# Scalings and operand making moved from ScalarE and GpSimd to VectorE, seven products reordered, loads reissued in another order

## Chip, cores and metric

One core of a Trainium2 chip. TensorE (PE) multiplies matrices, VectorE (DVE), ScalarE (ACT) and GpSimd (POOL) work elementwise, SyncE (SP) starts transfers. Each engine executes its own instructions strictly in the order in which they were written, and waits where an instruction's operands or its target are not ready. The metric is the device time of one execution in microseconds, the median of several runs; lower is better.

## What is computed

Four sequences, eight heads, 576 positions of 64 features go through causal attention with a memory term; its output, seen as 2304 rows of 512 features, goes through four experts, all of which act on every row, weighted by probabilities.

```
a = softmax(causal(scale * q @ k.T));  local = a @ v
mem_out = (phi(q) @ M_prev) / (phi(q) @ z_prev + 1e-6)
x = g * mem_out + (1 - g) * local          # rows: 4 x 576, features: 8 heads x 64
p = domain_probs / domain_probs.sum(-1)
out = sum over e of  p[:, e] * (relu(x @ w1[e]) @ w2[e])    # 512 -> 1024 -> 512
```

## The kernel before

Numbers are kept in fp32. A product of the experts is made of three matmuls: each operand is split into a high half (`...h`, rounded) and a low half (`...l`, what the rounding left), and high·high, low·high and high·low are summed. So every operand costs one rounding copy and one subtraction on some engine before PE can use it.

**Expert phases.** The four experts' weights come in 8 halves of 512 hidden features, and the kernel goes through them in 32 phases. In phases 0 to 23 one or two groups of 256 rows are resident. A phase first makes h = x @ w1 for four blocks `fc` of 128 hidden features (`mm1`: 12 matmuls a block), with relu on ACT (`hh`, L836) and the low half on DVE (`hl`, L837), then y = h @ w2 (`mm2`: 12 matmuls of 512 columns for 128 rows) and adds y into `acc`. The groups become resident as attention finishes them, so attention and phases are interleaved: attention's steps are sorted by (slot, priority), and a planner places them between the parts of the phases by costs.

**Attention.** The first run of eight heads is made ahead (`first_run`). Then twelve joint tasks (two heads, 256 query rows) of four slots each, and after them tasks of single heads. A task loads q, k and v (`t_load`, into one of two sets of `natall` that alternate from task to task), transposes them (`tk`, `tp` on PE), makes scores, subtracts the maximum, exponentiates, sums (`j_sum`, L497 and L500: 1/sum into `st`), scales the scores `s` by `st` (`j_norm`, L506), transposes them to `pt`, copies these to `pth` (ACT) and `ptl` (DVE, L527), and multiplies by v (`o`). The result goes through `otmp` (ACT) into `xr` (DVE).

**Weights.** `w_dma` fills one of four stage buffers `stg` on SP's queue, and waits there for the buffer to come free; `w_prep` makes of it the high half (ACT or POOL, L240 and L242) and the low half (POOL, in some phases DVE, L244), and calls `w_dma` for the next.

**Tail.** Phases 24 to 31 work on the last 1024 rows at once. x and w1 are cut into 2 x 2 blocks, and x @ w1 is made in seven products instead of eight. `x_ops` makes the seven left operands A11, S1, S2, A12, S3, S4, A22 (sums at L970, high halves on ACT at L962, low halves at L963), a step at a time between the parts of phases 22 and 23, where DVE and POOL both make odd and even low halves of weights too. `wt_prep` makes the right ones: four sums `tsum`, three high halves on ACT (L1000 to L1002), three low halves `wtl`. `tail_mm1` then runs the seven products in two halves p of a phase; each is six matmuls into a PSUM bank X, Y or Z, and later products are added into the bank's earlier sum. ACT keeps the first three in `trow`; then each add (L1041), relu (L1037) and `hl` or `xl` (L1038) gives one of four blocks of h. `tail_mm2` makes y from h: 96 matmuls (`yt`), in which a pair of row tiles takes blocks 0 and 2 of the hidden features first and blocks 1 and 3 after. The line that ties the products to the elementwise work in the kernel before is

```
add(product("A12", 1, "Z"), 0, 0, p)      # DVE add, then ACT relu, then DVE low half
add(product("S3", 5, "X"), 1, 1, p + 2)
```

Of the kernel before, what the change touches and what calls it, by code (L numbers as in the profile page):

```python
# [58 lines left out]
def tile_attention_moe(  # L59
# [145 lines left out]
    wpos = {"dma": 0, "prep": 0}  # L205
# [19 lines left out]

    def w_prep(i, kind, pool=False):
        last_ = PH0 - 3 <= i < PH0
        act = (kind == "1" or i < START[1] or last_) and not pool
        j = wpos["prep"]
        if j >= len(wseq) or wseq[j][0] != i or wseq[j][1] != kind:  # L230
            return
        wpos["prep"] += 1
        fc = wseq[j][2]
        t = stg.pop(j)
        hi, lo = (w1s if kind == "1" else w2s)[fc]
        if kind == "1":
            hi = hi.rearrange("p c f -> p (c f)")
            lo = lo.rearrange("p c f -> p (c f)")
        if act:
            nc.scalar.activation(hi, t, AF.Copy)  # L240
        else:
            nc.gpsimd.tensor_scalar(hi, t, 1.0, 1.0, ALU.mult, ALU.mult)  # L242
        dve = (last_ and fc % 2) or (i < START[1] and fc < PR["lod"])
        (nc.vector if dve else nc.gpsimd).tensor_tensor(lo, t, f(hi), ALU.subtract)  # L244
        w_dma()
# [48 lines left out]
    def t_load(t):  # L294
        for n, src, c0 in (("q", q, t.cs[0]), ("k", k, 0), ("v", v, 0)):
            nfull = min(t.nk, NCH - 1) - c0
            for j in range(2):
                s_ = src[t.b, 2 * t.a + j]
                nc.sync.dma_start(
                    out=t.nat[n][:, 0:nfull, j],  # L300
                    in_=s_[c0 * P : (c0 + nfull) * P].rearrange("(c p) d -> p c d", p=P),
                )
            if t.nk == NCH:
                for r in {"q": (D,), "k": (0,), "v": (0, D)}[n]:
                    nc.sync.dma_start(
                        out=t.nat[n][r : r + S - 4 * P, nfull],
                        in_=src[t.b, 2 * t.a : 2 * t.a + 2, 4 * P : S].rearrange(
                            "h p d -> p h d"
                        ),
                    )  # L310
# [191 lines left out]
    def j_norm(i):  # L502
        s = slots[i]
        r = s.st[:, 4:6]
        for hd in range(2):
            nc.scalar.activation(s.s3[:, hd], s.s3[:, hd], AF.Copy, scale=r[:, hd : hd + 1])  # L506
# [223 lines left out]
    for t in tasks:  # L730
# [7 lines left out]
        ev(ld, 8, lambda t=t: t_load(t))  # L738
# [10 lines left out]
    for i, s in slots.items():  # L749
        w = wid(s.c)  # L750
        t = s.t
        if t.joint:
            ev(i, PQ["qk"], lambda i=i: j_qk(i), 4 * mm(w))
            ev(i, PQ["exp"], lambda i=i: j_exp(i))
            ev(i + PQ["jn"][0], PQ["jn"][1], lambda i=i: j_sum(i))
            ev(i + PQ["jn"][0], PQ["norm"], lambda i=i: j_norm(i))
# [160 lines left out]
    tail = {}  # L917
# [37 lines left out]
    def x_ops():  # L955
# [9 lines left out]
        def plain(n, i, k):  # L965
            return [lambda: put(n, a_blk(i, k), nc.gpsimd)]

        def summed(n, eng, dst, a, b, op):
# [8 lines left out]
            + summed("S2", nc.vector, s_, s_, a_blk(0, 0), ALU.subtract)  # L977
            + plain("A12", 0, 1)
            + summed("S3", nc.gpsimd, s3, a_blk(0, 0), a_blk(1, 0), ALU.subtract)
            + summed("S4", nc.vector, s_, a_blk(0, 1), s_, ALU.subtract)  # L980
# [3 lines left out]
    def wt_prep(i):  # L984

        j = wpos["prep"]
        if j >= len(wseq) or wseq[j][0] != i or wseq[j][1] != "1":
            return
        wpos["prep"] += 2
# [5 lines left out]
        gp = nc.gpsimd.tensor_tensor  # L995
# [10 lines left out]
        w_dma()  # L1006
        w_dma()

    def tail_mm1(i, p):
# [25 lines left out]
        def done(src, blk, fc):  # L1035
            h_, l_ = tail["h"][blk][0][fc], tail["h"][blk][1][fc]
            nc.scalar.activation(h_, src, AF.Relu)  # L1037
            nc.vector.scalar_tensor_tensor(l_, src, 0.0, f(h_), ALU.max, ALU.subtract)  # L1038

        def add(o, n, blk, fc):  # L1040
            nc.vector.tensor_tensor(r[:, n], o, r[:, n], ALU.add)  # L1041
            done(r[:, n], blk, fc)
# [4 lines left out]
        add(product("A12", 1, "Z"), 0, 0, p)  # L1047
        add(product("S3", 5, "X"), 1, 1, p + 2)
        add(product("S4", 2, "Y"), 2, 0, p + 2)
        done(product("A22", 6, "X"), 1, p)  # L1050
# [387 lines left out]
```

## Time and profile before

| | |
|---|---|
| median of 3 runs | 1077.06 us (1076.23 to 1078.12) |
| the profiled execution | 1077.43 us, of which the span from its first to its last instruction 1075.5 |
| granted clock of TensorE, mean | 0.981 of full speed |
| PE, DVE, ACT, POOL busy | 1003.5, 654.3, 567.6, 544.5 us |
| phases 0 to 23 with attention | up to about 730 us |
| phases 24 to 31 (tail) | from there to the end |

Busy times add up what an engine's instructions took, so the engine with the largest share is near its limit, and the others wait for it or for each other. The table says nothing of where in time the waits stand; the views below do. In a view of waits, "PE o L541 <- DVE ptl L527" reads: PE stood at its instruction of line 541, which writes `o`, until DVE's instruction of line 527, which writes `ptl`, was done.

### The profile page before, as it was taken

The numbers are of one execution on the slowest core, as the hardware profiler recorded it, in microseconds if no ns is written. First come the engines' busy times: TensorE is split into PE (matmuls) and PEld (weight loads), VectorE is DVE, ScalarE is ACT, GpSimd is POOL, SyncE is SP. The second block draws the span as 40 slices with busy tenths as digits, with TensorE's granted clock in tenths as the row PEclk, the third lists the DMA queues.
The fourth block names the chain that finished last, engine by engine and source line by source line (L and its number), as shares of the span: only waits on it lengthen the run. The fifth ranks groups of instructions, "written<-read, shape, count | busy, mean of one in ns | idle before, by whom it ended". The sixth has DMA issues, their size and how long they took to land.

```text
span 1075.5 us, 15732 instructions
## 1 busy us (share of the span) xinstructions
PE 1003.5 (93%) x5072; PEld 827.8 (77%) x5072; DVE 654.3 (61%) x1555; ACT 567.6 (53%) x1299; POOL 544.5 (51%) x592
## 2 busy tenths in 40 slices
PE   5787889979999999999999999978999999999998
PEld 3576767768888788888878888856877877878776
DVE  5666766677677677777667776564444444533533
ACT  4476856767666666767656666543232241332320
POOL 4657765465465466546475354378325235235220
PEclk8999989999999999999999999979999999999999
DMA  6545653545454445335543342434111112112002
GB/s 135 121 123 152 163 142 96 131 122 139 104 131 112 110 106 153 105 108 129 150 110 92 102 105 85 119 98 118 51 47 60 40 46 72 40 40 79 24 16 78
DMA packets 192513, 106.33 MB, mean 99 GB/s; under 512 B 99632, under 2 KB 170800, under 8 KB 192432
## 3 DMA queue, kind: packets, MB, share of 16 engines
q1 hardware_dynamic: 191760, 105.07, 36.2%
q8 instruction: 40, 0.66, 0.3%
q10 hardware_dynamic: 672, 0.27, 0.1%
q14 instruction: 41, 0.34, 0.1%
HBM read 90.09 MB, written 4.72 MB: 88 GB/s over the span
## 4 chain that ended last, share of the span: by engine, by line
PE 69%; DVE 13%; ACT 6%; issue 4%; POOL 4%; DMA 2%; SPq 1%; POOLq 0%; DVEq 0%; ACTq 0%
PE yt L1063 16%; PE y L857 15%; PE h L827 13%; PE o L708 3%; PE tc_1X L1022 3%; PE sp L597 3%; PE tc_0X L1022 3%; PE pt L345 3%; DVE trow L1041 2%; DVE hl L837 1%; POOL w2l L244 1%; DVE hl L1038 1%; DMA natall<-in_k_dram 1%; ACT hh L836 1%; PE tc_0Z L1022 1%
## 5 line engine op out<-in xcount | busy, mean ns | idle before, releaser
L244 POOL TENSOR_TENSOR w1l<-stg,w1h 128x512 fp32r<-128x512 f32 x90 | 116.8, 1303 | 160.6 <-ACT w1h L240 153.3
L244 POOL TENSOR_TENSOR w2l<-stg,w2h 128x512 fp32r<-128x512 f32 x122 | 160.7, 1317 | 28.7 <-ACT w2h L240 17.7
L827 PE MATMUL h<-xh,w1h 128*128 128x512 f32 (+1 forms) x384 | 149.9, 390 | 0.0
L827 PE MATMUL h<-xh,w1l 128*128 128x512 f32 (+1 forms) x384 | 139.5, 363 | 3.1 <-POOL w1l L244 3.1
L857 PE MATMUL y<-w2h,hh 128*128 128x512 f32 x320 | 138.1, 432 | 0.8 <-ACT w2h L240 0.8
L827 PE MATMUL h<-xl,w1h 128*128 128x512 f32 (+1 forms) x384 | 138.8, 361 | 0.0
L857 PE MATMUL y<-w2l,hh 128*128 128x512 f32 x320 | 128.0, 400 | 3.9 <-POOL w2l L244 3.3
L857 PE MATMUL y<-w2h,hl 128*128 128x512 f32 x320 | 128.2, 401 | 0.9 <-DVE hl L837 0.9
L837 DVE SCALAR_TENSOR_TENSOR hl<-h,hh 128x512 fp32r<-128x512 f32 (+1 forms) x96 | 57.7, 601 | 83.7 <-ACT hh L836 83.0
L1076 DVE SCALAR_TENSOR_TENSOR xt<-yt,pn,xt 128x512 f32<-128x512 f32 x56 | 42.0, 751 | 80.8 <-PE yt L1063 80.8
L640 ACT ACTIVATE s<-s,st 128x384 f32<-128x384 f32 (+2 forms) x80 | 55.0, 688 | 66.5 <-DVE st L635 66.4
L242 POOL TENSOR_SCALAR w2h<-stg 128x512 fp32r<-128x512 f32 x100 | 63.5, 635 | 45.3 <-PE yt L1063 45.3
L827 PEld LDWEIGHTS h<-xh,w1l 128*128 128x128 f32 x384 | 74.5, 194 | 14.4 <-POOL w1l L244 3.3
L827 PEld LDWEIGHTS h<-xh,w1h 128*128 128x128 f32 x384 | 74.9, 195 | 6.5 <-issue 0.2
L827 PEld LDWEIGHTS h<-xl,w1h 128*128 128x128 f32 x384 | 75.1, 196 | 5.5
L857 PEld LDWEIGHTS y<-w2h,hl 128*128 128x128 f32 x320 | 61.1, 191 | 14.9 <-DVE hl L837 1.2
L857 PEld LDWEIGHTS y<-w2l,hh 128*128 128x128 f32 x320 | 61.6, 192 | 13.6 <-POOL w2l L244 5.4
L873 DVE SCALAR_TENSOR_TENSOR acc<-y,pn,acc 128x512 f32<-128x512 f32 x70 | 52.3, 747 | 30.1 <-PE y L857 29.1
L1003 POOL TENSOR_TENSOR wtl<-stg,wth 128x512 fp32r<-128x512 f32 x16 | 20.9, 1306 | 97.6 <-ACT wth L1000 97.6
L836 ACT ACTIVATE hh<-h 128x512 fp32r<-128x512 f32 (+1 forms) x96 | 50.3, 524 | 36.3 <-PE h L827 35.3
L857 PEld LDWEIGHTS y<-w2h,hh 128*128 128x128 f32 x320 | 61.5, 192 | 9.5 <-ACT w2h L240 1.3
L646 DVE TENSOR_TENSOR ptl<-pt,pth 128x384 fp32r<-128x384 f32 (+1 forms) x96 | 51.8, 553 | 20.4 <-ACT pth L644 19.7
(294 smaller groups left out, 2635.6 us busy)
## 6 DMA issues: line engine op xcount, KB each, us to landing
stg<-in_moe_w_dram SPq DMA_DIRECT2D x256, 256.0 KB, 2.9
natall<-in_k_dram SPq DMA_DIRECT2D x34, 128.0 KB, 2.8
natall<-in_v_dram SPq DMA_DIRECT2D x32, 128.0 KB, 2.6
natall<-in_q_dram SPq DMA_DIRECT2D x60, 64.0 KB, 2.6
out_dram<-acc SPq DMA_DIRECT2D x10, 256.0 KB, 2.2
kha<-kha SPq DMA_DIRECT2D x16, 128.0 KB, 3.4
khb<-khb SPq DMA_DIRECT2D x16, 128.0 KB, 3.2
natall<-in_k_dram SPq DMA_DIRECT2D x28, 64.0 KB, 2.5
```

What stands on the lines that cost most here:

```text
L242: nc.gpsimd.tensor_scalar(hi, t, 1.0, 1.0, ALU.mult, ALU.mult)
L244: (nc.vector if dve else nc.gpsimd).tensor_tensor(lo, t, f(hi), ALU.subtract)
L640: nc.scalar.activation(s.s[:, 0:w], s.s[:, 0:w], AF.Copy, scale=s.st[:, 3:4])
L646: lambda x=x: nc.vector.tensor_tensor(x[2], x[0], f(x[1]), ALU.subtract) for x in groups
L827: nc.tensor.matmul(pt[0][:, cols], lhsT=w_[:, c], rhs=x_[:, c, cols], start=(c == 0 and z == 0), stop=(c == NKD - 1 and z == 2),)
L836: nc.scalar.activation(h_, pt[0][:, cols], AF.Relu)
L837: nc.vector.scalar_tensor_tensor(l_, pt[0][:, cols], 0.0, f(h_), ALU.max, ALU.subtract)
L857: nc.tensor.matmul(pt[0], lhsT=h_[fc][:, tk], rhs=w_, start=(fc == 0 and z == 0), stop=(fc == HF - 1 and z == 2),)
L873: nc.vector.scalar_tensor_tensor(acc[g, tt], pt[0], pe, acc[g, tt], ALU.mult, ALU.add)
L1022: nc.tensor.matmul(bank[b][:, 0:TB], lhsT=w_[:, n, cs], rhs=x_[:, c], start=first and c == 0 and z == 0, stop=c == 1 and z == 2, skip_grou ...
L1063: nc.tensor.matmul(o, lhsT=h_[fc][:, tk], rhs=w_, start=(z == 0 and fc == p and y == 0), stop=(z == 1 and fc == p + 2 and y == 2),)
L1076: nc.vector.scalar_tensor_tensor(acc_, o, pe, acc_, ALU.mult, ALU.add)
```

## The change

- `j_norm`: the scaling of the joint scores is two tensor_scalar instructions on DVE, issued directly after `j_sum`, where it was two activations on ACT, issued later in the same slot.
- `x_ops`: the low halves of A11, A12 and A22 and both steps of S3 are made on DVE, where they were on POOL, and the operands are made in the order A11, S1, S2, S4, S3, A12, A22.
- `wt_prep` for phase 24 alone: the sums and the first `wtl` on DVE, where they were on POOL.
- `tail_mm1`: products in that order too; the relus are issued directly behind the adds, and the low halves later.
- Weight loads are counted as due when a preparation is issued, and issued ahead of the next preparation (`w_more`).
- `t_load` is called twice: for q and k at slot s0 − 9 of a task that starts at slot s0, for v at s0 − 7. Before, all three were loaded at s0 − 7 (s0 − 9 for the first task).

```diff
+    def w_more():
+        while wpos["due"]:
+            wpos["due"] -= 1
+            w_dma()
...
     def w_prep(i, kind, pool=False):
...
+        w_more()
         wpos["prep"] += 1
...
-        w_dma()
+        wpos["due"] += 1
...
-    def t_load(t):
+    def t_load(t, names="qkv"):
         for n, src, c0 in (("q", q, t.cs[0]), ("k", k, 0), ("v", v, 0)):
+            if n not in names:
+                continue
...
     def j_norm(i):
...
         for hd in range(2):
-            nc.scalar.activation(s.s3[:, hd], s.s3[:, hd], AF.Copy, scale=r[:, hd : hd + 1])
+            nc.vector.tensor_scalar(s.s3[:, hd], s.s3[:, hd], r[:, hd : hd + 1], None, ALU.mult)
...
-        ev(ld, 8, lambda t=t: t_load(t))
+        ev(s0 - 9, 8, lambda t=t: t_load(t, "qk"))
+        ev(ld, 8, lambda t=t: t_load(t, "v"))
...
-            ev(i + PQ["jn"][0], PQ["jn"][1], lambda i=i: j_sum(i))
-            ev(i + PQ["jn"][0], PQ["norm"], lambda i=i: j_norm(i))
+            ev(i + PQ["jn"][0], PQ["jn"][1], lambda i=i: (j_sum(i), j_norm(i)))
...
         def plain(n, i, k):
-            return [lambda: put(n, a_blk(i, k), nc.gpsimd)]
+            return [lambda: put(n, a_blk(i, k), nc.vector)]
...
+            + summed("S4", nc.vector, s_, a_blk(0, 1), s_, ALU.subtract)
+            + summed("S3", nc.vector, s3, a_blk(0, 0), a_blk(1, 0), ALU.subtract)
             + plain("A12", 0, 1)
-            + summed("S3", nc.gpsimd, s3, a_blk(0, 0), a_blk(1, 0), ALU.subtract)
-            + summed("S4", nc.vector, s_, a_blk(0, 1), s_, ALU.subtract)
             + plain("A22", 1, 1)
...
     def wt_prep(i):
...
+        w_more()
         wpos["prep"] += 2
...
-        gp = nc.gpsimd.tensor_tensor
+        gp = (nc.vector if i == PH0 else nc.gpsimd).tensor_tensor
...
-        w_dma()
-        w_dma()
+        wpos["due"] += 2
...
-        def done(src, blk, fc):
+        def relu(src, blk, fc):
+            nc.scalar.activation(tail["h"][blk][0][fc], src, AF.Relu)
+
+        def rest(src, blk, fc):
             h_, l_ = tail["h"][blk][0][fc], tail["h"][blk][1][fc]
-            nc.scalar.activation(h_, src, AF.Relu)
             nc.vector.scalar_tensor_tensor(l_, src, 0.0, f(h_), ALU.max, ALU.subtract)

-        def add(o, n, blk, fc):
+        def add(o, n):
             nc.vector.tensor_tensor(r[:, n], o, r[:, n], ALU.add)
-            done(r[:, n], blk, fc)
+            return r[:, n]
...
-        add(product("A12", 1, "Z"), 0, 0, p)
-        add(product("S3", 5, "X"), 1, 1, p + 2)
-        add(product("S4", 2, "Y"), 2, 0, p + 2)
-        done(product("A22", 6, "X"), 1, p)
+        c12 = add(product("S4", 2, "Y"), 2)
+        relu(c12, 0, p + 2)
+        c22 = add(product("S3", 5, "X"), 1)
+        relu(c22, 1, p + 2)
+        rest(c12, 0, p + 2)
+        c11 = add(product("A12", 1, "Z"), 0)
+        relu(c11, 0, p)
+        rest(c22, 1, p + 2)
+        c21 = product("A22", 6, "X")
+        relu(c21, 1, p)
+        rest(c11, 0, p)
+        rest(c21, 1, p)
```

Three places show how instructions move. On DVE in the first half of phase 24, what follows the products stood in the kernel before like this (`tc_0X` to `tc_0Z` are the banks):

```order
L1041 TENSOR_TENSOR trow<-tc_0Z,trow 128x512
L1038 SCALAR_TENSOR_TENSOR hl_111<-trow,hh_107 128x512
L1041 TENSOR_TENSOR trow<-tc_0X,trow 128x512
L1038 SCALAR_TENSOR_TENSOR xl<-trow,xh 128x512
L1041 TENSOR_TENSOR trow<-tc_0Y,trow 128x512
L1038 SCALAR_TENSOR_TENSOR hl_113<-trow,hh_109 128x512
L1038 SCALAR_TENSOR_TENSOR xl<-tc_0X,xh 128x512
```

In the changed kernel the same place reads:

```order
L1052 TENSOR_TENSOR trow<-tc_0Y,trow 128x512
L1052 TENSOR_TENSOR trow<-tc_0X,trow 128x512
L1049 SCALAR_TENSOR_TENSOR hl_113<-trow,hh_109 128x512
L1052 TENSOR_TENSOR trow<-tc_0Z,trow 128x512
L1049 SCALAR_TENSOR_TENSOR xl<-trow,xh 128x512
L1049 SCALAR_TENSOR_TENSOR hl_111<-trow,hh_107 128x512
L1049 SCALAR_TENSOR_TENSOR xl<-tc_0X,xh 128x512
```

The add that reads bank X has moved ahead of the first low half, and bank Z's add has moved from first to third.

On DVE in phases 22 and 23, between the second y of one phase (`acc_0`, `acc_1`) and the third low half of the next (`hl_113`), the kernel before had these rows:

```order
L873 SCALAR_TENSOR_TENSOR acc_0_6350<-y_4_0_8086,pn,acc_0_6350 128x512
L244 TENSOR_TENSOR w1l_118<-stg_8041,w1h_117 128x512
L873 SCALAR_TENSOR_TENSOR acc_1_6393<-y_4_1_8111,pn,acc_1_6393 128x512
L244 TENSOR_TENSOR w1l_122<-stg_8084,w1h_121 128x512
L970 TENSOR_TENSOR xsum<-xt,xsum 128x1024
L837 SCALAR_TENSOR_TENSOR hl_111<-h_0_8135,hh_107 128x256
L963 TENSOR_TENSOR S4l<-xsum,S4h 128x1024
L837 SCALAR_TENSOR_TENSOR hl_112<-h_1_8155,hh_108 128x256
L244 TENSOR_TENSOR w2l_126<-stg_8108,w2h_125 128x512
```

The changed kernel has these:

```order
L979 TENSOR_TENSOR xsum<-xt,xsum 128x1024
L882 SCALAR_TENSOR_TENSOR acc_0_6348<-y_4_0_8084,pn,acc_0_6348 128x512
L251 TENSOR_TENSOR w1l_118<-stg_8059,w1h_117 128x512
L972 TENSOR_TENSOR S4l<-xsum,S4h 128x1024
L979 TENSOR_TENSOR trow<-xt 128x1024
L882 SCALAR_TENSOR_TENSOR acc_1_6392<-y_4_1_8109,pn,acc_1_6392 128x512
L251 TENSOR_TENSOR w1l_122<-stg_8099,w1h_121 128x512
L972 TENSOR_TENSOR S3l<-trow,S3h 128x1024
L846 SCALAR_TENSOR_TENSOR hl_111<-h_0_8132,hh_107 128x256
L972 TENSOR_TENSOR A12l<-xt,A12h 128x1024
L846 SCALAR_TENSOR_TENSOR hl_112<-h_1_8153,hh_108 128x256
L251 TENSOR_TENSOR w2l_126<-stg_8124,w2h_125 128x512
```

The S4 sum has moved ahead of `acc_0`; S4's low half and the S3 sum now stand ahead of the odd low half `w1l_122`, and the low halves of S3 and A12 ahead of `hl_111` and `hl_112`.

On SP near the program's start, where the first joint tasks' loads stand (`kha`, `khb` and `qz` are copies within the chip), the kernel before had:

```order
L219 DMA stg_479<-in_moe_w_dram 128x4x128
L380 DMA kha_88<-kha_88 64x256
L380 DMA khb_89<-khb_89 64x256
L399 DMA qz_85<-qa_83 64x256
L399 DMA qz_85<-qb_84 64x256
L299 DMA natall<-in_q_dram 128x2x64 x2
L299 DMA natall<-in_k_dram 128x2x64 x2
L299 DMA natall<-in_v_dram 128x2x64 x2
```

The changed kernel has:

```order
L219 DMA stg_475<-in_moe_w_dram 128x4x128
L308 DMA natall<-in_q_dram 128x2x64 x2
L308 DMA natall<-in_k_dram 128x2x64 x2
L389 DMA kha_88<-kha_88 64x256
L389 DMA khb_89<-khb_89 64x256
L408 DMA qz_85<-qa_83 64x256
L408 DMA qz_85<-qb_84 64x256
L308 DMA natall<-in_v_dram 128x2x64 x2
```

q and k have moved ahead of the copies of the task before, and v has stayed behind them.

## Rows read from the trace of the kernel before

**Rows 1.** The page, busy time of each engine: us, share of the span, instructions.

```profile
PE 1003.5 (93%) x5072; PEld 827.8 (77%) x5072; DVE 654.3 (61%) x1555; ACT 567.6 (53%) x1299; POOL 544.5 (51%) x592
```

**Rows 2.** Stretches, busy us: PE, PEld, DVE, ACT, POOL; then clock, DMA share, GB/s.

```profile
44.00:240.00 196.00, 163.66 (x941) 138.15 (x939) 132.57 (x373) 133.72 (x365) 120.26 (x143) 0.97 0.49 130
240.00:684.00 444.00, 437.84 (x2327) 366.94 (x2328) 314.31 (x849) 294.71 (x670) 238.03 (x242) 1.00 0.43 114
684.00:756.00 72.00, 60.84 (x290) 49.82 (x289) 40.69 (x50) 32.68 (x57) 50.30 (x37) 0.88 0.38 114
718.20:722.00 3.80, 3.71 (x17) 3.72 (x18) 3.01 (x5) 2.65 (x4) 2.25 (x2) 0.50 0.48 152
```

**Rows 3.** Chain that ended last, phase 25: start us, us, what (xcount).

```profile
755.91 21.76 PE yt L1063 x96
...
779.03 1.36 PE tc_0Y L1022 x6
...
783.22 0.70 DVE trow L1041
...
784.60 1.08 DVE hl L1038
...
786.34 1.65 PE tc_0X L1022 x6
...
797.95 21.78 PE yt L1063 x96
```

**Rows 4.** PE's timeline, 718 to 737 us: start, us, instruction [idle before <-releaser].

```profile
718.29 0.58 PE L827 MATMUL h<-xh,w1l 128*128 128x256 f32 x1 [3.09 <-POOL w1l L244]
...
726.56 0.50 PE L857 MATMUL y<-w2l,hh 128*128 128x512 f32 x1 [1.06 <-POOL w2l L244]
...
736.61 0.50 PE L1022 MATMUL tc_0X<-S2h,wth 128*128 128x512 f32 x1 [3.16 <-ACT trow L1033]
```

**Rows 5.** POOL's timeline, 710 to 727 us.

```profile
710.64 2.39 POOL L970 TENSOR_TENSOR trow<-xt 128x1024 f32<-128x1024 f32 x1
...
722.22 2.62 POOL L963 TENSOR_TENSOR A22l<-xt,A22h 128x1024 fp32r<-128x1024 f32 x1 [1.76 <-ACT A22h L962]
...
727.28 0.74 POOL L997 TENSOR_TENSOR tsum<-stg,tsum 128x256 f32<-128x256 f32 x1
```

**Rows 6.** ACT's timeline at 735 us.

```profile
735.02 1.06 ACT L1002 ACTIVATE wth<-tsum 128x1024 fp32r<-128x1024 f32 x1 [3.69 <-POOL tsum L999]
```

**Rows 7.** DVE's timeline, 717 to 721 us.

```profile
717.03 2.28 DVE L970 TENSOR_TENSOR xsum<-xt,xsum 128x1024 f32<-128x1024 f32 x1
719.24 0.41 DVE L837 SCALAR_TENSOR_TENSOR hl<-h,hh 128x256 fp32r<-128x256 f32 x1
720.44 1.23 DVE L963 TENSOR_TENSOR S4l<-xsum,S4h 128x1024 fp32r<-128x1024 f32 x1 [0.79 <-ACT S4h L962]
```

**Rows 8.** Waits of PE, then of SP's queue, 40 to 240 us: total us, times, longest.

```profile
PE o L541 <- DVE ptl L527: 11.4, 7, 4.4
PE tk L345 <- DMA natall<-in_k_dram: 10.0, 5, 4.4
PE tp L345 <- DVE xr L568: 5.5, 5, 1.9
PE tp L345 <- ACT w2h L240: 2.4, 2, 1.5
...
SPq L224 <- POOL w1l L244: 29.7, 20, 3.8
```

**Rows 9.** ACT's scalings as a group (busy, mean ns, idle before); then their like on DVE in the first run.

```profile
L506 ACT ACTIVATE s<-s,st 128x128 f32<-128x128 f32 (+1 forms) x47 | 18.8, 447 | 32.4 <-DVE st L500 32.3
...
29.73 1.83 DVE L1200 TENSOR_SCALAR sf<-sf,stf 128x256 f32<-128x256 f32 x2
...
35.62 0.62 DVE L1200 TENSOR_SCALAR sf<-sf,stf 128x256 f32<-128x256 f32 x2
```

**Rows 10.** The chain inside 44 to 240 us, shares by line.

```profile
by line: PE y L857 9.8%; issue 8.3%; DMA natall<-in_k_dram 6.5%; PE h L827 6.1%; DVE ptl L527 3.8%; ACT hh L836 3.8%; DVE hl L837 3.7%; ACT s L506 3.7%; SPq L299 3.2%; DVE st L497 3.2%; DVE xr L568 2.8%; ACT otmp L555 2.7%; POOL w2l L244 2.
```

More of the change, by code (lines that the diff above doesn't have):

```diff
@@ L204, in tile_attention_moe @@
     NSTG = 4
-    wpos = {"dma": 0, "prep": 0}
+    wpos = {"dma": 0, "prep": 0, "due": 0}
     stg = {}
```

## The prediction

> **What bounds the kernel now.** I read the page's busy shares first, then busy times by stretch, then the chain of waits in the tail and the engines' waits inside the stretches that the change touches. TensorE (PE) is the bound: 93% busy, while VectorE (DVE) has 61% [rows 1]. So time comes only out of places where PE stands still, or runs at a lower granted clock after it stood. The stretches [rows 2] show where these are: from 240 to 684 us PE is busy 437.8 of 444.0 us at clock 1.00, and there is nothing to be had; from 44 to 240, where the joint slots run, it is idle 196.0 − 163.7 = 32.3 us, clock 0.97; from 684 to 756, where the operands of the products are made, it is idle 11.2 us, clock 0.88. In the tail after it the loss shows in the chain, since a matmul behind a wait is recorded longer and covers part of its idle time. I take tail, transition and early stage in turn. The profiled execution took 1077.43 us, 0.37 above the median of the runs; the sum is made against it.
>
> **Tail: products reordered, low halves deferred.** Each half phase shows the same chain [rows 3]: products of 1.36 us, and behind A12 an add on DVE (0.70), a relu on ACT, hl on DVE (1.08), the next add, and only then the seventh product. That product goes into bank X, which the second add must have read, and this add stands in DVE's queue behind hl, which waits for the relu. From the first add's start at 783.22 to the seventh product at 786.34 are 3.1 us; PE has two products (2.7) to do meanwhile, and the seventh takes 1.65 for 1.36. From yt at 755.91 to yt at 797.95 are 42.04 us. The work in them is 21.76 + 14 × 1.36 = 40.80, so 1.24 is lost in each of the six phases 25 to 30: 7.4. Phase 31 and the second half of phase 24 show the same chain; at a rounded 0.5 in each of their three halves they add 1.4. Together 8.8.
>
> In the new order the add behind S3 follows the add behind S4 directly. S3 ends 1.36 after S4, so the first add (0.70) is then done, and the second ends some 0.8 after S3, within A12's 1.36: A22 finds bank X read. What is late next is A12's low half. In a phase's second half it stands behind an add (0.70) and two hl (1.08 each), 2.9 with hops, or 3.5 if a relu delays one. Ahead of the first matmul of yt that reads it lie A22 (1.36) and 14 matmuls of 0.23 (21.76 / 96): 4.5 us. So I take the whole **−8.8**; with 0.2 left in each of 15 halves it is −6.
>
> **Transition.** Three PE waits are named there [rows 4]. Two are for low halves that POOL makes (3.09 and 1.06). POOL's rows [rows 5] say why: ahead of that w1l stand the S3 difference (2.39) and S3's low half, of A22l's shape (2.62), and ahead of the w2l stands A22l. The change takes all of these off POOL, so the low halves follow their high halves at once: −4.1. Right behind the first wait the clock is 0.50 for 3.8 us [rows 2], in which PE does half the work; with the wait this goes too: −1.9. The third wait (3.16) is for ACT's copy of a product, which stands behind wth at 735.02, and that waited 3.69 for POOL's sums [rows 6]. POOL's eight sums of 0.74 (5.9 us) and two wtl become DVE's: sums of 128x256 at 0.41 and wtl of twice their size at 0.82 [rows 7], so 2 × (4 × 0.41 + 0.82) = 4.9 in all. The sums alone end 8 × 0.33 = 2.6 sooner: −2.6; the copy still stands behind wth, so the rest of the wait stays.
>
> Against that DVE, busy 40.7 of 72.0 us [rows 2], takes on the 4.9, the low halves of A11, A12, A22 and S3 at 1.23 [rows 7], and the S3 difference. That has no row with POOL quiet: 2.28 beside POOL for the same shape [rows 7], 1.23 for another subtraction of that size; I take 1.3, as POOL has less to do. hl and odd low halves of the weights stand in the same queue: behind A11l (1.2) in phase 22, behind the S3 pair (2.5) and A12l and A22l (2.5) in phase 23. The last two lie under PE's 48 matmuls, half of the S3 pair too, so +2.5. Sum −4.1 − 1.9 − 2.6 + 2.5 = **−6.1**. Bounds: all 6.2 late, −2.4, or −1.4 with the S3 difference at 2.28; none late, −8.6.
>
> **Early stage (44 to 240).** PE's waits there [rows 8]: ptl 11.4, the k load 10.0, xr 5.5, w2h from ACT 2.4. (1) q and k are issued two slots earlier (some 8 us: twelve joint tasks of four slots each stand in 196 us), ahead of the v load, and weight loads no longer directly behind each preparation. SP starts transfers in order and is held 29.7 us by slots of w1 that POOL has not freed [rows 8]; q and k stood behind those. The 10.0 go. (2) ACT loses its scalings, 18.8 us, and the 32.3 us that its queue stood at them waiting for st [rows 9]. So w2h comes in time (−2.4), and xr, which waits on DVE for an ACT result, loses about half its wait (−2.7). (3) DVE gets 24 pairs of scalings. The same operation stands on DVE in the first run [rows 9]: a pair of 128x256 takes 0.62, or 1.83 where POOL is at work. I take 0.62 for the 128x128 pairs too, and POOL is busy 120.3 of 196 us, 61%: 24 × 0.62 + 12 × 0.61 × 1.21 = 23.7 us. So far DVE's 132.6 busy us make PE wait 11.4 + 5.5 = 16.9, 0.127 for one: 3.0 for the added ones. As its slack shrinks I double it: +6.0. Sum −10.0 − 2.4 − 2.7 + 6.0 = **−9.1**. Bounds: all 23.7 late against the 15.1, +8.6; none late and the clock back at 1.00 too (0.03 × 163.7 = 4.9), −20.
>
> The pair of rows 0.62 and 1.83 agrees with the Trainium skill, SBUF — State Buffer, section Who interferes with whom: a tensor_scalar in its two-port mode shares a port pair with GpSimd, and whoever issues first holds it for a whole instruction. That speaks against this part of the change; how often the two meet no page says.
>
> **Weight loads one preparation later: 0.** Each waits for a stage slot to come free, which is no later than before; the issue only moves past other transfers on SP's queue. In the tail eight loads have 42 us.
>
> **Sum.** 1077.43 − 8.8 − 6.1 − 9.1 = 1053.4; against the median, 1053.1. I say **1053.5**.
>
> **Rivals.**
> R1, the early stage gives nothing: DVE becomes its bound, and what k gives comes back as waits for ptl and xr. For it: ptl is the largest wait already, and DVE gets 23.7 us more. Against it: ACT's scaling (3.7%) and k's load (6.5%) stand on that stretch's chain [rows 10], 7.3 and 12.7 us. It gives 1077.4 − 14.9 = 1062.5.
> R2, slower: the scalings meet POOL nearly always, at 12 × (0.62 + 1.83) = 29.4 us, and stand on the chain in the place of ACT's 7.3, while k comes no sooner, as its landing buffer is not free sooner (SP's issue of these loads has 3.2% of the chain [rows 10]). Then 1077.4 − 14.9 + 22.1 = 1084.6. It decides from +17 us in this stretch on. Against it: POOL is idle 39% of it.
> R3, the transition gives nothing: DVE, with 40.7 + 4 × 1.23 + 1.3 + 4.9 = 51.8 of 72 us, takes POOL's place as what PE waits for: 1059.5.
> R4, more: half of PE's waits for DVE (16.9) go as well, the added scalings lie in DVE's idle time, and the clock comes back: 1053.4 − 6.0 − 8.5 − 4.9 = 1034.
> R5, no part does what it says: 1077. The tail's chain, adds and products alone, speaks against it.
>
> **Numbers.** Forecast 0.48, R1 0.22, R4 0.12, R3 0.10, R2 0.06, R5 0.02. The forecast's bounds, all three terms at one end, are 1040 and 1078; terms with different causes will hardly all lie there. 1043 to 1066 holds the forecast's middle, R1 and R3 with some room, and leaves out R4, R2 and R5, 0.20 together. About 0.2% (2.15 us) is what a measurement of this kernel tells from no change. R2 is slower, R5 the same: faster 0.92, same 0.02, slower 0.06.
>
> **What would show it.** Tail: a phase of 40.8 to 41.0 instead of 42.04, and no add in the chain; over 41.5 a hop or a bank was missed. Transition: no PE wait for POOL's w1l or w2l of over 0.5, the one for the copy under 1, and waits for hl or w1l of DVE of 2 to 4 instead. Early: no wait for k, scalings in pairs of 0.6 and 1.2 to 1.8, PE's waits for ptl and xr together 17 to 25. I am wrong if these rise beyond 30 (R1, R2), or if the wait for k stays near 10.

## The result, and the profile after

The changed kernel takes 1052.4 us (median of four runs, 1051.71 to 1052.46) against 1076.71 for the kernel before: a ratio of 0.9771, 95% interval 0.9754 to 0.9788, about 24.7 us less. The forecast was 1053.5 in a range of 1043 to 1066. The profiled executions differ by 1075.5 − 1050.6 = 24.9 us in span, and starts of the same work in both traces say where those lie (us from the span's start):

| from | before | after | length before | length after | difference |
|---|---|---|---|---|---|
| 0, to phase 22's first matmul | 693.54 | 684.58 | 693.54 | 684.58 | −8.96 |
| phase 22 | 711.92 | 704.61 | 18.38 | 20.03 | +1.65 |
| phase 23 | 730.54 | 716.98 | 18.62 | 12.37 | −6.25 |
| phase 24, first half of the products | 745.78 | 729.69 | 15.24 | 12.71 | −2.53 |
| second half | 755.74 | 739.21 | 9.96 | 9.52 | −0.44 |
| y of phase 24, phases 25 to 31 | 1075.5 | 1050.6 | 319.76 | 311.39 | −8.37 |

The second and third columns give where each part ends. Each side is one execution: kernels that leave the part ahead of phase 22 as it was spent 691.70 (`e1_tail`) and 695.47 us (`e2_ops`) on it, where the kernel before has 693.54, so the first row is known to some 2 us. The tail's two rows are −8.81 (forecast −8.8), the transition's three −7.13 (forecast −6.1), the early part −8.96 (forecast −9.1). Three sums so near their forecasts would suggest that each reason is right. The experiments show that two of the three are not, in part.

The page's busy times after the change. PE does the same instructions in 6.6 us less recorded time, since fewer of them stand behind a wait or run at the low clock; DVE has taken 29.6 us [rows 1].

```profile
PE 996.9 (95%) x5072; PEld 829.0 (79%) x5072; DVE 683.9 (65%) x1618; ACT 552.8 (53%) x1251; POOL 522.1 (50%) x577
```

The same stretches as [rows 2], the later ones cut at the corresponding places of the program (columns as there):

```profile
44.00:240.00 196.00, 174.93 (x1005) 148.31 (x1004) 164.41 (x444) 126.18 (x337) 126.10 (x150) 0.97 0.54 141
240.00:675.00 435.00, 427.59 (x2263) 359.43 (x2263) 307.65 (x826) 285.19 (x649) 234.11 (x238) 1.00 0.42 111
675.00:739.40 64.40, 56.76 (x289) 47.01 (x288) 48.05 (x65) 33.79 (x58) 26.69 (x22) 0.92 0.41 127
```

From 44 to 240 us PE's idle time went from 32.3 to 21.1 us, and DVE's busy time from 132.6 to 164.4. Those 31.8 are more than the scalings, since the stretch now holds more of the program. Around the transition POOL's work fell from 50.3 to 26.7 us.

The chain over a tail phase, against [rows 3]: it is products alone, no add and no low half, and from yt to yt are 780.17 − 739.37 = 40.80 us, exactly the sum of the matmuls, where it was 42.04.

```profile
739.37 21.76 PE yt L1082 x96
761.13 1.36 PE tc_0X L1031 x6
...
778.81 1.36 PE tc_1X L1031 x6
780.17 21.76 PE yt L1082 x96
```

PE's waits in the early stage, against [rows 8]: k is gone, ptl and xr are down from 16.9 to 9.7 (I had said 17 to 25), and a wait for POOL's low half of w2 is up from 1.1 (first line, of the kernel before) to 5.4.

```profile
PE y L857 <- POOL w2l L244: 1.1, 2, 0.9
...
PE o L550 <- DVE ptl L536: 7.0, 7, 2.1
PE y L866 <- POOL w2l L251: 5.4, 4, 3.3
PE tp L354 <- DVE xr L577: 2.7, 2, 1.6
PE y L866 <- DVE st L506: 2.1, 2, 1.2
```

And PE's timeline in the transition, against [rows 4]. The wait of 3.09 for POOL's w1l is gone. The wait for ACT's copy is 2.50 where it was 3.16 (I had said under 1). Waits of 0.99 and 0.79 for POOL's w2l are left, where I had said none over 0.5. In phase 22 a low half of w2 that DVE makes now holds PE 1.62; the same place took 0.61 before (first line).

```profile
706.82 0.80 PE L857 MATMUL y<-w2l,hh 128*128 128x512 f32 x1 [0.61 <-DVE w2l L244]
...
693.10 0.49 PE L866 MATMUL y<-w2l,hh 128*128 128x512 f32 x1 [0.99 <-POOL w2l L251]
...
698.47 0.80 PE L866 MATMUL y<-w2l,hh 128*128 128x512 f32 x1 [1.62 <-DVE w2l L251]
...
712.96 0.50 PE L866 MATMUL y<-w2l,hh 128*128 128x512 f32 x1 [0.79 <-POOL w2l L251]
...
722.75 0.50 PE L1031 MATMUL tc_0X<-S2h,wth 128*128 128x512 f32 x1 [2.50 <-ACT trow L1042]
```

### The profile page after: what moved, and what is told of

Read it like the earlier page. It is cut to its first block, busy times and chain, and to the rows that moved or that the text cites. A ratio compares the mean times of both kernels' runs of the same rounds, so it can differ in the third digit from the quotient of the medians.

```text
span 1050.6 us, 15677 instructions
## 1 busy us (share of the span) xinstructions
PE 996.9 (95%) x5072; PEld 829.0 (79%) x5072; DVE 683.9 (65%) x1618; ACT 552.8 (53%) x1251; POOL 522.1 (50%) x577
## 4 chain that ended last, share of the span: by engine, by line
PE 76%; DVE 12%; ACT 5%; DMA 2%; issue 2%; SPq 1%; POOL 1%; ACTq 0%; DVEq 0%; POOLq 0%
PE y L866 17%; PE yt L1082 17%; PE h L836 13%; PE tc_1X L1031 4%; PE tc_0X L1031 4%; PE o L717 4%; PE sp L606 3%; PE pt L354 3%; PE tc_1Y L1031 2%; PE tc_0Y L1031 2%; DVE hl L846 1%; PE tc_1Z L1031 1%; PE tc_0Z L1031 1%; DVE kl L382 1%; ACT hh L845 1%
## 5 line engine op out<-in xcount | busy, mean ns | idle before, releaser
L354 PE MATMUL pt<-ident,s 128*128 128x128 f32 (+1 forms) x376 | 61.2, 274 | 2.2 <-DVE s L515 1.6
```

The lines of the kernel that those rows point to most:

```text
L354: nc.tensor.transpose(dst, src, ident[0:n, 0:n])
```

## Experiments

My theory is the forecast's sum: tail −8.8, operands −6.1, q and k −10, scalings +0.9, weight loads 0, each by itself. The rivals are that DVE's new work eats what the loads give (R1), and that the parts depend on each other, so that a part's worth is not what it gives alone. I tried each part by itself on the kernel before, then the whole change without one part, then two variants of the scaling, and last two changes that the traces suggested. Ratios are against the kernel before on the same chip, with their 95% intervals; 0.001 is 1.08 us. The runs stand on several chips, so kernels are compared with each other by these ratios.

**One part at a time.** `e1_tail` has only the new `tail_mm1`:

```diff
-        add(product("A12", 1, "Z"), 0, 0, p)
...
+        c12 = add(product("S4", 2, "Y"), 2)
+        relu(c12, 0, p + 2)
...
+        rest(c21, 1, p)
```

> The kernel before with the new order of products and the deferred low halves in the seven-product halves alone. My sum: -8.8 us (0.7 to 0.9 per cent), a phase of 40.8 instead of 42.04. Rival: part of that gain needs the operands made elsewhere (the first half waits for ACT's copy anyway), then -8.4 or less; a rival by which bank or relu waits take the gain would show 0 to -4.

Measured: 0.9914 (0.990 to 0.9929), −9.3 us, the forecast inside the interval of 7.6 to 10.8. The chain has the new period with all else as before: 793.88 − 753.08 = 40.80.

```profile
753.08 21.76 PE yt L1073 x96
...
793.88 6.35 PE yt L1073 x28
```

So this part needs none of the others, and its reason is shown: the second add no longer stands behind a low half.

`e2_ops` has only the operands on DVE, in the new order:

```diff
-            return [lambda: put(n, a_blk(i, k), nc.gpsimd)]
+            return [lambda: put(n, a_blk(i, k), nc.vector)]
...
+            + summed("S4", nc.vector, s_, a_blk(0, 1), s_, ALU.subtract)
+            + summed("S3", nc.vector, s3, a_blk(0, 0), a_blk(1, 0), ALU.subtract)
             + plain("A12", 0, 1)
-            + summed("S3", nc.gpsimd, s3, a_blk(0, 0), a_blk(1, 0), ALU.subtract)
-            + summed("S4", nc.vector, s_, a_blk(0, 1), s_, ALU.subtract)
...
-        gp = nc.gpsimd.tensor_tensor
+        gp = (nc.vector if i == PH0 else nc.gpsimd).tensor_tensor
```

> The kernel before with the operands of the last pass (left operands, and the right ones of its first phase) made on VectorE in the new order, products in the old order. My sum: -6.1 us, of it -4.1 from the waits for POOL's low halves, -1.9 clock, -2.6 from the sums, +2.5 from low halves late on VectorE; the trace of the whole change shows -7.1 over the same stretch, part of which (0.3 to 0.6) is the first half's product order. Rival: VectorE only takes POOL's place, 0.

Measured: 0.9987 (0.9976 to 0.9999), −1.4 us, far from −6.1. In its trace the wait for w1l is gone, as forecast, but the wait for ACT's copy has grown to 3.98. The sums before it, at 0.41 to 0.42 us in the first set, are longer in the second, on DVE:

```profile
730.46 0.42 DVE L997 TENSOR_TENSOR tsum<-stg,tsum 128x256 f32<-128x256 f32 x1
730.80 0.83 DVE L998 TENSOR_TENSOR tsum<-stg 128x256 f32<-128x256 f32 x1
731.56 1.48 DVE L999 TENSOR_TENSOR tsum<-stg,tsum 128x256 f32<-128x256 f32 x1
732.96 1.09 DVE L1003 TENSOR_TENSOR wtl<-stg,wth 128x512 fp32r<-128x512 f32 x1
```

In the same stretch POOL makes the next w2, which it can since the loads came at once:

```profile
730.49 0.87 POOL L242 TENSOR_SCALAR w2h<-stg 128x512 fp32r<-128x512 f32 x1 [7.13 <-DMA stg<-in_moe_w_dram]
731.45 1.31 POOL L244 TENSOR_TENSOR w2l<-stg,w2h 128x512 fp32r<-128x512 f32 x1
732.72 0.79 POOL L242 TENSOR_SCALAR w2h<-stg 128x512 fp32r<-128x512 f32 x1
```

The sum of 1.48 us starts at 731.56, just behind POOL's w2l of 731.45 (1.31), and ends at 733.04, 0.3 behind the end of that row. So the part that I had costed at 0.41 for each sum meets POOL after all, in the way of the 0.62 and 1.83 of [rows 9], and I had costed the sums as if POOL were idle. In the same trace phases 22 and 23 take 31.94 us for 37.00, so the operands by themselves give 5.1 there. The first half of phase 24 takes 16.54 for 15.24, 1.3 more, and the part ahead of phase 22, which this edit doesn't touch, was 1.9 longer in this execution.

`e3_qk` has only the split load:

```diff
-        ev(ld, 8, lambda t=t: t_load(t))
+        ev(s0 - 9, 8, lambda t=t: t_load(t, "qk"))
+        ev(ld, 8, lambda t=t: t_load(t, "v"))
```

> The kernel before with q and k loaded two slots earlier alone; weight loads still directly behind each preparation, scalings on ACT. My sum gives the k wait's 10.0 us to this part, with the weight loads' place counted as nothing: -10 (or about -6.6 if only the two longest waits, 4.41 and 2.21, are worth their time). Rival: without the later weight loads q and k still stand behind them in SP's queue, or the time comes back as other waits: 0 to -3.

Measured: 0.9888 (0.9867 to 0.9910), −12.1 us. No wait for k is left, and with it went over a third of those for ptl and xr, of which I had given this part nothing: together 9.5, where the kernel before has 16.9 [rows 8], `e1_tail` 15.2 and `e2_ops` 15.5. Nothing but the loads differs, so they had been late because q and k were. ACT's w2h, though, is waited for as before (2.4 in [rows 8]).

```profile
PE o L543 <- DVE ptl L529: 6.2, 7, 1.8
PE tp L347 <- DVE xr L570: 3.3, 5, 1.1
PE tp L347 <- ACT w2h L240: 2.1, 2, 1.7
```

The later weight loads, which I had named as part of the reason, are not needed for it. And the 10.0 us that I had read for k are those of one execution. `e1_tail` (first line) and `e2_ops` (second), which leave the early stage as it was, show less:

```profile
PE tk L345 <- DMA natall<-in_k_dram: 6.6, 3, 4.4
PE tk L345 <- DMA natall<-in_k_dram: 6.4, 3, 4.0
```

`e4_norm` has only `j_norm` on DVE, in one step with `j_sum`:

```diff
-            nc.scalar.activation(s.s3[:, hd], s.s3[:, hd], AF.Copy, scale=r[:, hd : hd + 1])
+            nc.vector.tensor_scalar(s.s3[:, hd], s.s3[:, hd], r[:, hd : hd + 1], None, ALU.mult)
...
-            ev(i + PQ["jn"][0], PQ["jn"][1], lambda i=i: j_sum(i))
-            ev(i + PQ["jn"][0], PQ["norm"], lambda i=i: j_norm(i))
+            ev(i + PQ["jn"][0], PQ["jn"][1], lambda i=i: (j_sum(i), j_norm(i)))
```

> The kernel before with the joint scalings on VectorE, directly behind the sums, alone. My sum: +6.0 for VectorE's added 23.7 us, -2.4 and -2.7 for what ACT serves sooner: +0.9 (-5 to +8). Rival A: VectorE is the early stage's bound, so some 10 or more us slower. Rival B: the scalings lay on the chain on ACT (3.7 per cent of 196 us, 7.3) and lie off it on VectorE: -5 to -7.

Measured: 0.9926 (0.9902 to 0.9949), −8.0 us, near rival B and outside the −5 to +8 of my sum. The waits that fell are some of those that `e3_qk` takes away too: ptl and xr together 8.3, where kernels with the old early stage have 15.2 to 16.9. The 5.8 for k is little less than the 6.4 of `e2_ops`. Whether the engine or the new place in the order gave the 8 was not tried on the kernel before.

```profile
PE o L541 <- DVE ptl L527: 6.1, 7, 2.3
PE tk L345 <- DMA natall<-in_k_dram: 5.8, 4, 4.3
PE y L856 <- POOL w2l L244: 3.6, 4, 1.6
...
PE tp L345 <- DVE xr L568: 2.2, 3, 0.9
```

`e5_due` has only the later weight loads:

```diff
...
-        w_dma()
+        wpos["due"] += 1
...
```

> The kernel before with the weight loads issued one preparation later alone. My sum counts this as nothing: within 0.2 per cent of the kernel before. Rival: what the loads no longer hold up on SP's queue (q, k, copies of k) comes sooner in the early stage: -2 to -6 us. Rival on the other side: weights arrive later in the early stage, where preparations stand close together: +2 to +5.

Measured: 0.9996 (0.9984 to 1.0008): nothing, as forecast.

The five add up to −9.3 − 1.4 − 12.1 − 8.0 − 0.4 = −31.2, the whole is −24.7. So they overlap somewhere and help each other elsewhere.

**Pairs, and the whole without one part.** `e6_ops_due` puts the diffs of `e2_ops` and `e5_due` together:

> The operands on VectorE together with the later weight loads, nothing else changed. In the run of the operands alone the second set of right operands of phase 24 took VectorE 0.83, 1.48, 1.09 and 1.49 us where the whole change shows 0.42, 0.42, 0.68 and 0.42, because GpSimd already made the next w2 from loads that had come sooner. Theory: the later loads keep GpSimd away from these rows, which then are short again, so that this kernel gains 2 to 3.5 us on the operands alone (-3.5 to -5 in all). My prediction's zero for the loads: the same as the operands alone, -1.4.

Measured: 0.9945 (0.9926 to 0.9963), −5.9 us: 4.5 more than the operands alone and 4.1 more than the two apart added up. The rows that were stretched are short again, and POOL's first w2h stands behind them, at 731.42:

```profile
728.77 0.42 DVE L1006 TENSOR_TENSOR tsum<-stg 128x256 f32<-128x256 f32 x1
...
729.45 0.69 DVE L1011 TENSOR_TENSOR wtl<-stg,wth 128x512 fp32r<-128x512 f32 x1
...
731.42 0.94 POOL L249 TENSOR_SCALAR w2h<-stg 128x512 fp32r<-128x512 f32 x1 [11.75 <-DMA stg<-in_moe_w_dram]
```

What each is worth in time is less plain. In the two profiled executions the wait for ACT's copy is 2.50 here and 3.98 in `e2_ops`, yet from phase 22's start to the second half's this kernel takes 49.2 us and the other 48.5: here the clock stays at 0.50 for 6 us behind the wait, and the seventh product waits 1.01. The spans of these two executions differ by 2.0 only, and that lies ahead of phase 22 (2.4). That the later loads keep POOL off these rows is shown; that this alone is worth 4.5 us is not.

`e8_no_due` is the whole change with `w_dma()` again directly behind each preparation.

```diff
...
-        w_more()
...
-        wpos["due"] += 1
+        w_dma()
...
```

> The whole change with weight loads directly behind each preparation as before. Theory: the transition loses the shelter from GpSimd's early w2 (2 to 3.5 us slower there); the early stage, where the whole change shows new waits of 5.4 us for GpSimd's low halves, gets its weights as early as before (up to 3 us faster). My prediction: the same as the whole change within 0.2 per cent.

Measured: 0.9802 (0.9780 to 0.9823), 3.3 us slower than the whole change; the two intervals overlap by a little. The stretch from phase 22 to the second half takes 48.99 us instead of 45.11. All of it lies in the first half of phase 24, 16.67 for 12.71: DVE's sums are stretched as in `e2_ops`, PE's wait for the copy is 3.99 again, and the clock is 0.80 there instead of 1.00.

```profile
719.22 1.48 DVE L1001 TENSOR_TENSOR tsum<-stg,tsum 128x256 f32<-128x256 f32 x1
...
722.33 0.79 PE L1024 MATMUL tc_0X<-S2h,wth 128*128 128x512 f32 x1 [3.99 <-ACT trow L1035]
```

The part ahead of phase 22 was 1.85 us shorter in this execution, which is no more than executions of the same code differ. In the transition the sign is as the theory had it, and the zero that I had given the loads, right by itself, is wrong beside operands that DVE makes.

`e7_no_norm` is the whole change with `j_norm` as before: on ACT, and a step of its own.

```diff
-            nc.vector.tensor_scalar(s.s3[:, hd], s.s3[:, hd], r[:, hd : hd + 1], None, ALU.mult)
+            nc.scalar.activation(s.s3[:, hd], s.s3[:, hd], AF.Copy, scale=r[:, hd : hd + 1])
...
-            ev(i + PQ["jn"][0], PQ["jn"][1], lambda i=i: (j_sum(i), j_norm(i)))
+            ev(i + PQ["jn"][0], PQ["jn"][1], lambda i=i: j_sum(i))
+            ev(i + PQ["jn"][0], PQ["norm"], lambda i=i: j_norm(i))
```

> The whole change with the joint scalings left on ACT as before. q and k sooner gave -12.0 us alone and the scalings -8.0 alone, but the whole early stage gains about 9. Theory A: once k comes in time, the scalings on VectorE only cost (their 24 us meet GpSimd): 2 to 3 us faster than the whole change. Theory B: both still add up in part, and something else takes the time back: 3 to 6 us slower than the whole change. My prediction's +6.0 - 2.4 - 2.7: 1 us faster.

Measured: 0.9734 (0.9715 to 0.9754), 4.0 us faster than the whole change, as theory A. The transition takes the same 45.12 us, and the part ahead of it ends 4.3 us sooner. So beside early q and k the scalings' part costs 4 us, where alone it gave 8. The parts ahead of phase 22 bear it out: 678.78 to 680.64 us in `e3_qk`, `e7_no_norm`, `e11_late_wth` and `e12_late_spread`, which have early q and k and the scalings on ACT in the old place, and 684.58 in the whole change.

**Engine or place.** That part does two things: it changes the engine, and it makes the scaling one step with the sum, earlier in each engine's queue and one step less in the planner's count. `e9_dve_old_place` and `e10_act_new_place` separate them, in the whole change.

```diff
-            ev(i + PQ["jn"][0], PQ["jn"][1], lambda i=i: (j_sum(i), j_norm(i)))
+            ev(i + PQ["jn"][0], PQ["jn"][1], lambda i=i: j_sum(i))
+            ev(i + PQ["jn"][0], PQ["norm"], lambda i=i: j_norm(i))
```

> The whole change with the joint scalings on VectorE, but issued as a step of their own at their old place in the slot (priority 2.3). The run with the scalings left on ACT was 4 us faster than the whole change; engine and place changed together there. Theory of place: the sums and scalings made one step let the planner set attention's later steps sooner, so GpSimd's memory operands (eight rows, 3.5 us) stand ahead of a low half of w2 that PE waits 3.33 us for; this kernel is then some 4 us faster than the whole change (ratio 0.973 to 0.974). Theory of the engine: VectorE's added 24 us, which meet GpSimd, cost the 4; this kernel is as the whole change (0.977).

The other has the diff of the engine alone:

```diff
-            nc.vector.tensor_scalar(s.s3[:, hd], s.s3[:, hd], r[:, hd : hd + 1], None, ALU.mult)
+            nc.scalar.activation(s.s3[:, hd], s.s3[:, hd], AF.Copy, scale=r[:, hd : hd + 1])
```

> The whole change with the joint scalings on ACT, in the new place directly behind the sums, in one step with them. Theory of place: as the whole change, 0.977 or slower. Theory of the engine: as the run with the scalings left on ACT, 0.973.

| scaling | old place | new place |
|---|---|---|
| on ACT | 0.9734 (0.9715 to 0.9754) | 0.9919 (0.9902 to 0.9937) |
| on DVE | 0.9731 (0.9701 to 0.9762) | 0.9771 (0.9754 to 0.9788), the whole change |

In the old place the engine makes no difference that the runs show, which leaves room for some 4 us. The new place costs 4.3 us with DVE and 20 with ACT. With DVE the intervals of the two places overlap by a little, but the traces agree: the part ahead of phase 22 takes 679.20 us in `e9_dve_old_place`, as with ACT, and 684.58 in the whole change. So the theory of place holds, and that of DVE's added work falls: DVE has all 24 pairs in `e9_dve_old_place` too, in 22.3 us. Part of why ACT suffers more in the new place stands in its own rows: it stands at the scalings 15.1 + 24.7 = 39.8 us for st, which DVE makes, against 28.9 in the old place of `e7_no_norm`, and everything behind in ACT's queue stands with it. That these 10.9 make the 20 is not shown.

```profile
L515 ACT ACTIVATE s<-s,st 128x256 f32<-128x256 f32 x24 | 10.9, 501 | 15.1 <-DVE st L509 15.1
L515 ACT ACTIVATE s<-s,st 128x128 f32<-128x128 f32 x24 | 8.3, 394 | 24.7 <-DVE st L509 24.7
```

On DVE it never waits (0.4 us of idle time before it in the whole change), so the 4 us there have another path. The one that I had named is not it alone. In the whole change eight POOL rows of the memory operands stand ahead of a w2l that PE then waits 3.33 us for, at 90.37 us; but `e9_dve_old_place` has such a wait too, 2.75 us at 107.18, behind three other POOL rows:

```profile
107.18 0.50 PE L867 MATMUL y<-w2l,hh 128*128 128x512 f32 x1 [2.75 <-POOL w2l L251]
```

Whether the 4 us come from the place in DVE's queue or from the planner, which counts one step less and so sets the later ones sooner, these runs don't separate.

**Two changes that the traces suggested**, both on `e7_no_norm`. PE's wait of 2.50 is left because ACT's copies stand behind the second set's last high half. `e11_late_wth` makes that half (`wth[3:7]`, the first `late` on ACT), and its low half (the second, on DVE), between the products instead:

```diff
...
         keep(product("S2", 4, "X"), 2)
+        late = tail["late"] if p == 0 else []
+        if late:
+            late.pop(0)()
         c12 = add(product("S4", 2, "Y"), 2)
         relu(c12, 0, p + 2)
+        if late:
+            late.pop(0)()
```

> The whole change with scalings left on ACT, and the last high and low half of phase 24's second set of right operands made behind the third copy of a product instead of ahead of the first. The 2.50 us that PE waits for ACT's copy, which stands behind that high half, should go, since the copies then follow their products: 2.5 us faster than without it (ratio 0.971). Rival: VectorE's adds of the first half now stand behind the late low half (1.23), and the seventh product waits instead: 1 us or nothing.

Measured: 0.9716 (0.9694 to 0.9738), a median of 1046.11 us. The wait is gone from PE's timeline, and the first half takes 721.24 − 711.14 = 10.10 us where `e7_no_norm` has 12.76: −2.66, the forecast.

```profile
711.14 0.39 PE L1042 MATMUL tc_0X<-A11h,wth 128*128 128x512 f32 x1
...
714.27 0.39 PE L1042 MATMUL tc_0X<-S2h,wth 128*128 128x512 f32 x1
...
721.24 0.39 PE L1042 MATMUL tc_1X<-A11h,wth 128*128 128x512 f32 x1
```

Of that 0.63 is lost again at once: the second half takes 10.15 for 9.52. Between the ratios lie 1.9 us, less than their intervals; the gain is shown by the trace, not by the times.

`e12_late_spread` also spreads the operand steps:

```diff
...
-                if z % 3 == 2 and pieces:
+                if z % 4 == 2 and pieces:
```

> As the run with the late second half, and the steps that make the left operands stand behind every fourth part of phases 22 and 23 instead of every third. In the second products of phase 22 PE waits 0.99, 0.92, 0.75 and 1.62 us for low and high halves that stand behind these steps on GpSimd, VectorE and ACT: with more room between the steps 1 to 3 us faster than without the spreading. Rival: the waits only move into phase 23, whose second products now wait for the same queues: nothing, or slower by 1 to 2.

Measured: 0.9714 (0.9694 to 0.9734), the same. In the trace phases 22 and 23 take 709.63 − 680.31 = 29.32 us against 32.36 in `e11_late_wth`, so the expected 1 to 3 us are there (the clock in phase 22 is 1.00 here and 0.75 there); in this execution the part ahead of them was 1.5 longer. The times don't tell the two apart. Either is 0.6% below the whole change (0.9716 and 0.9714 against 0.9771, intervals apart), so both beat both kernels.

## Why the prediction was right, point by point

**The tail** was right in mechanism and size: −8.8 forecast, −8.8 in the trace, −9.3 alone. The period is the sum of the matmuls, and the 0.2 in each half that the bound of −6 allowed for did not come. (Three halves at 0.5 are 1.5, where the sum has 1.4.)

**The transition** was right in sum (−6.1 against −7.1), and part of that is luck. Phases 22 and 23 together take 32.40 us for 37.00, −4.6, where my terms for them give −4.1 − 1.9 + 2.5 = −3.5. PE's waits there for POOL fell by 3.5 and those for DVE rose by 1.0, so DVE's added work cost less than I had; PE's recorded busy time, which holds the lower clock, fell by 2.1. How the gain falls on the two phases is no fixed thing: +1.65 and −6.25 here, but `e9_dve_old_place`, with the same code in them, spends 18.84 and 13.49.

The first half gained 2.53 where I had 2.6, but not by my reason, that the sums end 2.6 sooner. ACT's last high half starts 721.16 − 716.98 = 4.18 us after the phase's first product, where it was 735.02 − 730.54 = 4.48 [rows 6], since the second set's sums now stand on DVE behind phase 23's last `acc`, at 718.92. So PE's wait fell by 0.66 only.

```profile
721.16 1.06 ACT L1012 ACTIVATE wth<-tsum 128x1024 fp32r<-128x1024 f32 x1 [2.25 <-DVE tsum L1009]
```

The rest is the new order of the products, 0.60 alone in `e1_tail`, and the clock, which fell to the lower of its two levels (0.50, 1.2 GHz) behind the wait in the kernel before and stayed at 1.00 in the changed one. Below is the first half in the kernel before, in `e4_norm` (same code in it), in the whole change and in `e9_dve_old_place` (same code as the whole change):

```profile
730.54:745.78 15.24, 11.78 (x44) 8.78 (x42) 7.08 (x8) 4.68 (x8) 13.67 (x15) 0.89 0.48 138
722.72:736.60 13.88, 10.20 (x43) 7.65 (x42) 6.96 (x8) 4.67 (x8) 12.31 (x14) 1.00 0.45 132
716.98:729.69 12.71, 10.13 (x43) 7.68 (x42) 9.23 (x16) 6.03 (x10) 6.50 (x7) 1.00 0.52 163
711.53:725.71 14.18, 11.60 (x44) 8.78 (x42) 9.29 (x16) 5.76 (x10) 7.79 (x8) 0.88 0.53 159
```

At the same clock the two codes differ by 13.88 − 12.71 = 1.2 us, and one code by 1.4 to 1.5 between the clocks. Why the clock falls in one execution and not in another, behind the same wait of 2.50, stays open.

The other step that failed is "Weight loads one preparation later: 0". I argued that a slot is free no later and that the tail has time. Both may hold; but a later load also makes POOL start later, and POOL's start was what the sums on DVE could not bear (`e2_ops`, `e8_no_due`). My prices of 0.41 for these sums were prices with POOL quiet, and the loads are what made it quiet. R3, DVE in POOL's place, did not come: the operands by themselves gave only 1.4 in time, but 5.1 in phases 22 and 23 of their trace.

**The early stage** was right in sum (−9.1 against −9.0) by errors that cancel. q and k were worth 12.1 alone, not 10.0, since ptl and xr were late in their wake; and the 10.0 was one execution's wait, of which others with the same early stage have 6.4 to 6.6. Of the two terms for ACT's relief, xr's came with q and k (3.3 for 5.5 in `e3_qk`), without any relief of ACT. The −2.4 for w2h did not: that wait is still 2.1 in `e3_qk` and `e7_no_norm` and is gone where DVE scales. But `e9_dve_old_place`, where DVE scales too, is no faster than `e7_no_norm`, so the runs show no time for it. The scalings, +0.9 in my sum (+6.0 − 2.4 − 2.7), cost 4.0 beside early q and k. The size of DVE's work was right (24.0 us in the rows below, 23.7 forecast), its make-up was not: I had 12 × 0.62 = 7.4 for the 128x128 pairs and 16.3 for the others, and they took 14.7 and 9.3. The step that failed is PE's wait of 0.127 us for each us of DVE, doubled, +6.0: in the old place the same work on DVE costs nothing that the runs show, and what costs is the place in the order, to which I had given no term.

```profile
L515 DVE TENSOR_SCALAR s<-s,st 128x128 f32<-128x128 f32 (+1 forms) x48 | 24.0, 541 | 0.8
```

**Rivals.** R1 did not come, but its idea, that k's gain would come back as waits, holds in part: three parts worth 12.1, 8.0 and 0.4 apart give 9.0 together. R2's price, 29.4 us on the path, did not come: DVE's scalings took 24.0, and on no path that the waits show beyond 1.6 us. R4 did not come: PE's waits for ptl and xr fell by 7.2, near the 8.5 that it has, but those for POOL's w2l rose by 4.3, and the clock stayed at 0.97.

## What to carry to other kernels

A sum that comes out right is no proof of its terms: price each part of a change by a run of that part alone and of the whole without it. When elementwise work moves to another engine, ask which engine works beside it at that moment and which transfer sets that moment; and when two steps of a scheduled program are joined, treat the new place in the queues as a change of its own. Where a late load delays a chain, the waits behind it are likely late with it: they go with the load, and should not be booked to another edit.

## What the runs showed of the hardware that was not expected

In the whole change the smaller scalings took longer: 24 of 128x128 took 14.7 us (651 ns each) and 24 of 128x256 took 9.3 (431 ns); single ones range from 272 to 1335 ns, the longest about as long as one of POOL's low halves (1.30 to 1.32 us in the mean). In the old place they took 10.7 and 11.6 us.

```profile
L515 DVE TENSOR_SCALAR s<-s,st 128x128 f32<-128x128 f32 x24 | 14.7, 651 | 0.4
L515 DVE TENSOR_SCALAR s<-s,st 128x256 f32<-128x256 f32 x24 | 9.3, 431 | 0.4
```

What POOL does beside them decides more than their size. A pair of 128x128 with no POOL instruction beside it took 0.48 us; one that started beside two of POOL's low halves took 2.32 and ended at 78.25, 0.07 behind them:

```profile
75.93 2.32 DVE L515 TENSOR_SCALAR s<-s,st 128x128 f32<-128x128 f32 x2
75.64 2.54 POOL L251 TENSOR_TENSOR w1l<-stg,w1h 128x512 fp32r<-128x512 f32 x2
...
202.81 0.48 DVE L515 TENSOR_SCALAR s<-s,st 128x128 f32<-128x128 f32 x2
```

Sums that read two operands show the same (1.48 for 0.42 us). That agrees with the Trainium skill, SBUF — State Buffer, section Who interferes with whom, in which an operation of VectorE in a two-port mode contends with GpSimd and the one that issues later is blocked for the whole instruction, and one with two inputs in SBUF contends with a GpSimd instruction that reads SBUF.
